# Attention, routing and two feed-forward layers in one kernel: start-up transfers, row numbers and the order of VectorE's work

## The chip, the cores and the metric

The kernel runs on one core of a Trainium2 chip. The metric is the device time of one execution in microseconds, the median of several runs. The engines are TensorE (PE in the profile, its weight loads PEld), VectorE (DVE), ScalarE (ACT), GpSimd (POOL) and SyncE (SP). SP and POOL also issue the DMA transfers, SP on a hardware queue (q1), POOL on a software queue (q0). Each engine carries out its list of instructions in order, and a waiting instruction holds all that stand behind it on its engine.

## What is computed

```python
# attention: 4 x 8 heads, 576 tokens, head size 64
scores = q @ k^T / 8 + min(-(cum_i - cum_j), 0), causal     # cum = cumsum(max(s, 0))
x = softmax(scores) @ v                                     # -> 2304 tokens x 512
# first layer: 8 experts, each takes at most 288 tokens
logits = x @ w_gate                                         # 2304 x 8
for idx in argsort(-logits.flatten()):                      # best pairs first
    give the token to the expert, if the token is free and the expert has room
x[tokens of e] = relu(x[tokens of e] @ w1[e]) @ w2[e]       # 512 -> 1024 -> 512
# second layer
h = x @ w_in                                                # 512 -> 2048
out = (h * sigmoid(1.702 h)) @ w_out                        # 2048 -> 512
```

## The kernel before, in words

**Attention.** The 32 heads go through a pipeline written out by hand in `SEQ`: in step i (`steps`), head i+1 gets its scores (`scores`, L165 and L174), head i its maxima, exponentials and first transposes, head i-1 its product with V (`av`, L228), head i-2 its projection (`fin`, L256). Scores are made of two passes, for more than one float32r's worth of digits. The first uses `X0`: the high part of K (`Ak` on ScalarE, L115, or `k` on POOL, L102) against the high and the low part of Q (`Aq` on ScalarE, L113, and `ql` on POOL, L104). The second uses 68 rows of `X1`: the low part of K (`kl`, POOL, L106), the high part of Q (`Aq1`, or `q1`, a transfer on SP, L108), and four rows 64 to 67 that add the bias: two hold running sums (`c`, two transfers of rows of `c_rows` on SP, L110 and L111) and two hold the constants 1 and -1. There are six such `X1` (`HS`), all in one tile `x1`. The constants are set once for head 0 (L312, L313) and copied to heads 1 to 5 by a POOL transfer (`rest`, L317 and L318). Two more POOL transfers bring `w_gate` into `fold` (L341).

Q and K of two heads are one `load(j)` (four transfers, L79), V of two heads one `load_v(j)` (L85). `prep(i)` issues the V load, `c`, `k`, `kl` and the split of V into a high and a low part (`split_v`, POOL, L91 and L92); `high(i)` issues the rest of head i and, for odd i, the Q and K of a later pair. From head 8 on this is done five steps ahead; the table `HIGH` gives the steps for heads 2 to 7. In the opening block (L304 to L347) the program's order holds on all five engines, in the steps on PE, ACT and DVE; elsewhere the framework's planner orders an engine's list by its own costs and by when it expects an instruction's inputs.

**Routing and experts.** A serial stretch decides which token goes where and leaves the row numbers `ids` (96 x 24). `output_rows` (L768) turns them into rows of the output: `orow` (L769 to L772), converted to whole numbers in `oidx` (L773), written to `o_rows` in memory (L774), and, once program order comes to expert 2, read back transposed as `oids` (128 x 18, L982), as the scatters at the end (L1080) want them. What follows on SP is kept behind the write by `issue_after`. The experts' weights come by `load_w` on SP (L506, L507) and are split on ACT and DVE (L781, L782); `up` (L898) and `down` (L908) multiply; `gather_t` (L873) transposes the gathered tokens of the next expert. Beside them run the conversions of `w_in` and `w_out` from 64-bit numbers (`from_f64`, L803 to L818): a load on SP (L805), then two half conversions on DVE, L808 and L812 (with L811 on ACT), and L814 and L817.

**Feed-forward.** Unit q = 0 to 71 is a chunk of 256 tokens and one of four column pairs; the first 36 units use the first half of the weights. Unit q makes h (`ff_in`, L1013), sg on ACT (L1024), g on DVE (L1025), four sums (L1031), gT's high part on ACT (L1219) and its low part on DVE (L1223). `ff_out` (L1045) multiplies into the banks y0 to y3; while q is below `DEEP` = 30 it does so for unit q-2. After each fourth product `rows_out` empties the banks: p1, p3, p4 are copied by ACT (L1112), and c11, u2, u3, u4, c22 are DVE's (L1076); c11 and u2 need p1. They are placed by slots, run in this order within a deep unit: "B", then g and the sums, gT's high part, "a", "A", gT's low part, "c". The remaining half conversions (`step`) stand in the same slots, one in a unit with p = 1 (that is where a chunk's products end) and two in the others. In the deep part p1 is in "a", c11, u2 and u3 in "A" behind the half conversion, u4 and c22 in "B" of the next unit.

The line that sets the conversions' slots, and the ones that set the sums':

```python
for slot in {1: "A", 2: "BA", 3: "BA", 0: "BA"}[p]:                                        # L1172
at(q, "A", add(c11, c11 if last else p1, P_[2]), add(u2, p1, P_[6]), add(u3, u2, P_[7]))   # L1113
at(q + 1, "B", add(u4, u2, P_[5]), add(c22, c22 if last else u3, P_[5]))                   # L1114
```

Zero matmuls (`pulse`, L691, on a tile `zeros`) already stand in the routing stretch, where TensorE would be idle.

Of the kernel before, what the change touches and what calls it, by code (L numbers as in the profile page):

```python
# [19 lines left out]
I32 = mybir.dt.int32  # L20
# [22 lines left out]
def f32(ap):  # L43
    return ap.bitcast(F32)
# [3 lines left out]
def tile_kernel(ctx, tc, qt, kt, v, s, w_gate, w1, w2, w_in, w_out, out):  # L48
# [33 lines left out]
    def load_v(j):  # L82
        t = att.tile([P, 2, T, D], F32, name="vraw", bufs=3)
        for r in (slice(0, 112), slice(112, P)):
            SY.dma_start(t[r].rearrange("p g t d -> p (g t d)"), v[j, r])  # L85
        st["v", j] = t
# [212 lines left out]
    wg = w_gate.rearrange("(h d) e -> d h e", d=D)  # L299
    sums = consts.tile([P, 5, T, 2], F32, name="sums")  # L300
    warm = consts.tile([1, 2], F32, name="warm")
    G.memset(warm, 0.0)
    with (tc.manual_schedule(engines={PE.engine, A.engine, V.engine, SY.engine, G.engine})):

        SY.dma_start(cs, s)
        first_raw = st["raw", 0] = att.tile([128, 2, 2, SP], F32, name="raw", bufs=3)
        for i in range(2):
            for n, src in ((0, qt), (1, kt)):
                for r in (LO, UP):
                    SY.dma_start(first_raw[r, n, i], src[0, i])  # L310
        A.activation(warm, warm, AF.Exp)
        G.memset(f32(x1[64:68, 0, 0]), 1.0)  # L312
        V.memset(f32(x1[64:68, 0, 1]), -1.0)  # L313
        G.memset(sc, 1.0)
        G.memset(sc[LO, 0:1], 0.125)
        G.memset(sc[UP, 1:2], 0.125)
        rest = f32(x1[64:68, 1:]).rearrange("p i n s -> p i (n s)")  # L317
        G.dma_start(rest, f32(x1[64:68, 0]).rearrange("p n s -> p (n s)")[:, None, :].to_broadcast(list(rest.shape)))  # L318
        G.memset(sums, 1e-9)

        V.tensor_scalar(cs, cs, 0.0, None, op0=OP.max)
        V.tensor_tensor_scan(c_sum, cs, cs, 0.0, op0=OP.add, op1=OP.max)
        A.activation(chl[:, 0], c_sum, AF.Copy)
        V.tensor_scalar(identf, jp, 0.0, None, op0=OP.is_equal)
        V.tensor_tensor(chl[:, 1], c_sum, f32(chl[:, 0]), op=OP.subtract)
        for h in range(2):
            SY.dma_start(f32(X1[h][66:68, 0]), f32(chl[h:h + 1]))
            SY.dma_start(f32(X1[h][64:66, 1]), f32(chl[h:h + 1]))
        SY.dma_start(c_rows, f32(chl))
        for what in ("Aq", "Ak", "Aq1", "Vql", "Vkl"):  # L330
            part(what, 0)
        V.tensor_scalar(identb, jp, 0.0, None, op0=OP.is_equal)
        V.tensor_scalar(maskb, jp, 0.0, -1e9, op0=OP.is_gt, op1=OP.mult)
        for what in ("Aq", "Ak", "Aq1", "Vql", "Vkl"):
            st["prep", 1] = part(what, 1)
        V.tensor_tensor(fold[:, :, :D], identf[:, None, :D].to_broadcast([128, H, D]),
                        identf[:, None, D:].to_broadcast([128, H, D]), op=OP.add)
        load(1)
        load_v(0)
        for g in range(2):  # L340
            G.dma_start(fold[g * D:(g + 1) * D, :, D:], wg)  # L341
        part("c", 2)
        prep(3)
        load(2)
        load_v(1)
        prep(2, False)
        load(3)  # L347

    FN = dict(S=lambda i, u: scores(i, u) if i else scores(0, u, (1,), False), M=row_max, X=exps, T=transp, H=p_hi, L=p_lo, A=av, O=av_out, N=norm, R=recip, F=fin, G=fin_out)

    HIGH = {2: 0, 3: 0, 4: 1, 5: 1, 6: 2, 7: 2}

    def steps(i0, i1):
        for i in range(i0, i1):
# [12 lines left out]
    att_engines.enter_context(tc.manual_schedule(engines={PE.engine, A.engine, V.engine}))  # L367
    for u in (2, 1, 0):
        scores(0, u, (0,))
    steps(-3, 14)  # L370

    zeros = keep.tile([128, 128], BF, name="zeros")
    late = ExitStack()
    late.enter_context(tc.issue_after(st["prep", 17].ins))
    G.memset(zeros, 0.0)
    jrow = rt.tile([128, 128], F32, name="jrow")
    G.iota(jrow, pattern=[[1, 128]], base=0, channel_multiplier=0, allow_small_or_imprecise_dtypes=True)
    pcol = rt.tile([128, 1], F32, name="pcol")
# [380 lines left out]
                fill_slots(False)  # L759


    orow = rt.tile([JS, NC], F32, name="orow")
    late = rt.tile([JS, NC], F32, name="late")
    oidx = keep.tile([JS, NC], I32, name="oidx")
    o_rows = dram.tile([N, 1], I32, name="o_rows")
    oids = keep.tile([128, N // 128], I32, name="oids")

    def output_rows():  # L768
        start = V.scalar_tensor_tensor(orow, ids[:, 1], float(P), ids[:, 0], op0=OP.mult, op1=OP.add)  # L769
        for b in range(1, B):  # L770
            V.tensor_scalar(late, ids[:, 1], float(b * T), float(S - SP), op0=OP.is_ge, op1=OP.mult)
            V.tensor_tensor(orow, orow, late, op=OP.add)  # L772
        V.tensor_copy(oidx, orow)  # L773
        ins = SY.dma_start(o_rows.rearrange("(c p) o -> p (c o)", p=JS), oidx)  # L774
        return start, ins


    JM0, JM, JM7, PM = (3, 3, 4, 4, 5, 5, 7, 7), (1, 1, 3, 3, 5, 5, 7, 7), tuple(m for m in range(1, 9) for _ in range(3)), 5
# [172 lines left out]
    for e in range(E):  # L951
        py = [bank(f"y{d}")[:, :CAP] for d in range(4)]
        hs = {}
        for m in range(10):
            if m < 8:
                if e == m == 0:
                    hs[m] = up(e, m)
                    ctx.enter_context(tc.issue_after(last_lo[0].ins))
                if m % 2 == 0:
                    g = m // 2 + 1  # L960
                    if g < 4:
                        ws[e, g] = weights(e, g)
                    elif e + 1 < E:
                        ws[e + 1, 0] = weights(e + 1, 0)
                if m not in hs:
                    hs[m] = up(e, m)
            if m == 1 and e + 1 < E:
                gather(e + 1)
            for _ in range((JM0 if e == 0 else JM7 if e == E - 1 else JM).count(m)):
                f = next(jobs_, None)  # L970
                if f:
                    f()
            if m == 6 and e + 1 < E:
                gather_t(e + 1)
            if m >= 2:
                down(e, m - 2, hs[m - 2], py)
        for d in range(4):
            A.activation(yt[:, d], py[d], AF.Copy)
        SY.dma_start(y_dram[:, :, e * CAP:(e + 1) * CAP], yt)
        yt = new_yt()  # L980
        if e == 2:
            SY.dma_start(oids, o_rows.rearrange("(c p) o -> p (c o)", p=128))  # L982
        if e in (0, 1):
            for f in load_y(e, wp):
                f()
# [82 lines left out]
    def at(q, slot, *fs):  # L1068
        todo.setdefault((q, slot), []).extend(fs)
# [18 lines left out]
    def rows_out(q, c, acc, last):  # L1088
# [21 lines left out]
            return  # L1110
        for o, k, slot in ((p1, 1, "a"), (p3, 3, "c"), (p4, 4, "c")):
            at(q, slot, lambda o=o, k=k: A.activation(o, P_[k], AF.Copy))  # L1112
        at(q, "A", add(c11, c11 if last else p1, P_[2]), add(u2, p1, P_[6]), add(u3, u2, P_[7]))  # L1113
        at(q + 1, "B", add(u4, u2, P_[5]), add(c22, c22 if last else u3, P_[5]))  # L1114
        if not last:
            at(q + 1, "A", add(c12, u4, p3), add(c21, u3, p4, OP.subtract))
            return
# [43 lines left out]
    with tc.manual_schedule(engines={PE.engine, A.engine, V.engine}):  # L1161
        for q in range(NQ):
# [5 lines left out]
            if p == 0 and 1 <= c < 2 * NCH - 1:  # L1168
                hi, lo = load_y(c + 1, fp)
                at(q + 1, "c", hi)  # L1170
                at(q + 2, "B" if c == NCH - 1 else "A", lo)
            for slot in {1: "A", 2: "BA", 3: "BA", 0: "BA"}[p]:  # L1172
                if q:
                    at(q, slot, lambda q=q: step(q))
            if 0 <= k + 2 < PP:
# [45 lines left out]
                do(q, "a")  # L1221
            do(q, "A")
            V.tensor_tensor(t[:, 1, :n], src, f32(t[:, 0, :n]), op=OP.subtract)  # L1223
            gs[q] = t
            do(q, "c")
        ends.pop()()
# [44 lines left out]
```

## Time and profile before

| what | us |
|---|---|
| median of 3 runs | 897.05 (896.64 to 898.61) |
| the profiled execution | 896.56 |
| its span, first to last instruction | 894.8 |
| mean granted TensorE clock | 0.973 of full speed |
| busy: PE / DVE / ACT / POOL | 840.4 / 723.6 / 509.0 / 276.8 |

The profile is of one execution. Its rows name an engine, a line of the kernel, an operation, the tile written and the tile read, how many such instructions there are and how long they took; brackets tell how long the engine had been idle ahead of the instruction and what ended that. Times of the timeline count from the first instruction. The granted clock is 1.00 for 2.4 GHz and 0.50 for 1.2 GHz.

### The profile page before, as it was taken

What the parts mean: (1) busy time and instruction counts of PE and PEld (TensorE: products, weight loads), DVE (VectorE), ACT (ScalarE), POOL (GpSimd) and SP (SyncE); (2) the same over time, 40 slices, a digit from 0 to 9 for tenths busy, and PEclk for the clock granted to TensorE, in tenths of its full rate; (3) what the DMA queues carried; (4) which work ended last, traced back from release to release, by engine and by line L of the source; (5) the groups of instructions that cost most, each with busy time, mean ns of one, the idle gap of its engine ahead of it and who ended that gap; (6) DMA issues with size and microseconds to landing.
All of it is one profiled execution on the core that took longest, in us unless ns stands there. A gap on an engine that the chain in (4) does not pass through costs nothing.

```text
span 894.8 us, 18574 instructions
## 1 busy us (share of the span) xinstructions
PE 840.4 (94%) x6853; PEld 821.0 (92%) x6853; DVE 723.6 (81%) x1683; ACT 509.0 (57%) x1141; POOL 276.8 (31%) x263
## 2 busy tenths in 40 slices
PE   4799999999669899999999999999999999999996
PEld 3699999999538899999999999999999999999996
DVE  4678889888777689999897798899978977777775
ACT  5889998997534557666664343434335434444442
POOL 2999999983242111021100011111010111111112
PEclk9899999999769999999999999999999999999999
DMA  6886558620346689888874333323256111111101
GB/s 160 193 199 167 149 136 217 156 75 6 123 146 104 226 243 280 258 270 248 258 236 181 99 118 101 118 83 111 73 189 222 56 49 48 48 48 49 48 24 49
DMA packets 88391, 124.38 MB, mean 139 GB/s; under 512 B 10541, under 2 KB 56769, under 8 KB 87781
## 3 DMA queue, kind: packets, MB, share of 16 engines
q1 hardware_dynamic: 85156, 113.55, 43.4%
q0 software_dynamic: 3136, 9.57, 3.7%
q8 instruction: 57, 0.93, 0.4%
q14 instruction: 42, 0.34, 0.1%
HBM read 96.61 MB, written 22.21 MB: 133 GB/s over the span
## 4 chain that ended last, share of the span: by engine, by line
PE 48%; DVE 12%; issue 4%; ACT 3%; DMA 2%; POOL 1%; SPq 0%; POOLq 0%; DVEq 0%; ACTq 0%
PE h L1013 13%; PE y L1045 11%; PE y L908 11%; PE h L898 11%; DVE g L1031 3%; DVE gT L1223 3%; ACT gT L1219 2%; DVE g L1025 2%; DVE part L1076 1%; PE h L873 1%; DVE tmp L1076 1%; DMA wi_dram<-wist 1%; DVE u L814 1%; DMA raw<-in_moe_w_in_dram 1%; DVE yc L941 1%
## 5 line engine op out<-in xcount | busy, mean ns | idle before, releaser
L1013 PE MATMUL h<-yc,win 128*128 128x256 f32 x1728 | 218.6, 283 | 0.0
L1013 PEld LDWEIGHTS h<-yc,win 128*128 128x128 f32 x1728 | 212.4, 192 | 0.0
L1045 PE MATMUL y<-wout,gT 128*128 128x256 f32 x1491 | 189.6, 282 | 7.0 <-DVE part L1076 3.9
L1045 PEld LDWEIGHTS y<-wout,gT 128*128 128x128 f32 x1491 | 180.9, 189 | 9.7 <-issue 4.2
L1219 ACT ACTIVATE gT<-g 128x896 fp32r<-128x896 f32 x72 | 68.4, 950 | 140.5 <-DVE g L1031 139.6
L908 PE MATMUL y<-hT,w2s 128*128 128x288 f32 x768 | 115.8, 299 | 0.0
L898 PE MATMUL h<-xT,w1s 128*128 128x288 f32 (+2 forms) x776 | 114.2, 295 | 0.0
L908 PEld LDWEIGHTS y<-hT,w2s 128*128 128x128 f32 x768 | 107.4, 191 | 0.0
L898 PEld LDWEIGHTS h<-xT,w1s 128*128 128x128 f32 x776 | 106.5, 188 | 0.1
L217 DVE TENSOR_TENSOR phl<-pt,phl 116x464 fp32r<-116x464 f32 (+1 forms) x128 | 76.2, 599 | 28.0 <-ACT phl L212 27.9
L1223 DVE TENSOR_TENSOR gT<-g,gT 128x896 fp32r<-128x896 f32 x72 | 78.9, 1096 | 16.4 <-ACT gT L1219 16.3
L1031 DVE TENSOR_TENSOR g<-g 128x128 f32<-128x128 f32 x284 | 75.2, 306 | 4.9
L228 PE MATMUL pt<-phl,vhl 116*128 116x232 f32 (+2 forms) x512 | 75.7, 291 | 2.4 <-POOL vhl L92 2.1
L212 ACT ACTIVATE phl<-pt 116x464 fp32r<-116x464 f32 (+1 forms) x128 | 69.2, 541 | 12.4 <-PE pt L206 12.1
L670 POOL DMA_INDIRECT xg<-x_rows,idx x24 | 29.3, 1222 | 141.2 <-PE h L873 134.8
L228 PEld LDWEIGHTS pt<-phl,vhl 116*128 116x128 f32 x512 | 66.4, 194 | 4.0 <-POOL vhl L92 2.8
L1080 POOL DMA_INDIRECT out_dram<-part,oids x18 | 22.2, 1231 | 150.5 <-DVE part L1076 150.5
L1020 ACT ACTIVATE sg<-h 128x256 f32<-128x256 f32 x84 | 32.1, 384 | 64.1 <-PE h L1013 63.5
L206 PE MATMUL pt<-identf,pr 116*116 116x116 f32 x480 | 66.7, 271 | 0.9 <-DVE phl L217 0.7
L1021 DVE TENSOR_TENSOR g<-h,sg 128x256 f32<-128x256 f32 x84 | 35.5, 423 | 32.9 <-ACT sg L1020 32.3
L165 PE MATMUL sc<-x 128*116 128x348 f32 (+3 forms) x192 | 44.8, 342 | 16.0 <-ACT x L115 10.4
L206 PEld LDWEIGHTS pt<-identf,pr 116*116 116x116 f32 x480 | 52.5, 143 | 4.4 <-PE sc L174 1.0
(199 smaller groups left out, 1433.6 us busy)
## 6 DMA issues: line engine op xcount, KB each, us to landing
wraw<-in_moe_w_dram SPq DMA_DIRECT2D x60, 512.0 KB
yraw<-y_dram SPq DMA_DIRECT2D x18, 512.0 KB
raw<-in_qt_dram SPq DMA_DIRECT2D x30, 290.0 KB
raw<-in_kt_dram SPq DMA_DIRECT2D x30, 290.0 KB
raw<-in_moe_w_in_dram SPq DMA_DIRECT2D x32, 256.0 KB
raw<-in_moe_w_out_dram SPq DMA_DIRECT2D x32, 256.0 KB
y_dram<-yt SPq DMA_DIRECT2D x8, 576.0 KB
vraw<-in_v_dram SPq DMA_DIRECT2D x16, 280.0 KB
```

The costliest lines, as they stand in the source:

```text
L165: PE.matmul(p[:, c0:c0 + w], X[x][:, 0, t * P:(t + 1) * P], X[x][:, 1, k0:k0 + w], start=x == 0 and banks[m] not in banks[:m], stop=x == 1 ...
L206: PE.transpose(p[:, w - P:w], pr[:, place(t, c):place(t, c + 1)], identf[:P, :P])
L212: A.activation(hl[:, 0], p, AF.Copy)
L217: st["lo", i] = V.tensor_tensor(hl[:, 1], st["pt", i, g], f32(hl[:, 0]), op=OP.subtract)
L228: PE.matmul(p[:, t0 * P:(t0 + n) * P], vhl[:, hh, c].rearrange("p a d -> p (a d)"), st["phl", i, g][:, x, col:col + n * P], start=x == 0 a ...
L898: PE.matmul(p[:, o], w[:, a, k, c], x[:, b, k, o], start=n == 0 and (e, m) != (0, 0), stop=n == len(steps) - 1)
L908: PE.matmul(py[d], w[:, a, m % 2, d * 128:(d + 1) * 128], h[:, b], start=m == 0 and n == 0, stop=m == 7 and n == 2)
L1013: PE.matmul(h, w[:, a, k], yc[c][:, b, k], start=n == 0 and (both is None or half == 0), stop=n == 11 and (both is None or half == 1))
L1031: V.tensor_tensor(g[:, o], g[:, a], g[:, b], op=op)
L1045: PE.matmul(acc[b][:, o * 256:o * 256 + 256], t[:, j, x], wout[:, p, i, y], start=p == 0 and n == 0 and b not in banks[:m], stop=end and n ...
L1219: A.activation(t[:, 0, :n], src, AF.Copy)
L1223: V.tensor_tensor(t[:, 1, :n], src, f32(t[:, 0, :n]), op=OP.subtract)
```

## The change

The constants are now set for two heads at once, and the transfer that copies them to the other four, with the two `w_gate` transfers, stands on POOL behind an element copied from V of pair 0, which it thus waits for. `HIGH` moves heads 3, 5 and 7 by a step. Zero matmuls are put on TensorE in two places, 12 at the start and 6 behind the first pass of head 0. The row numbers stay float32, are transposed on TensorE before they are written and after they are read back (through a spent tile, `lg_all`), and their write stands at expert 0's seventh round, behind `gather_t(1)`. In the feed-forward two slots are added: "e" takes u4 and c22 and "z" takes the half conversion of p = 1, both behind gT's low part; c11, u2 and u3 go to the front of "A".

```diff
+    zeros = keep.tile([128, 128], BF, name="zeros")
+    G.memset(zeros, 0.0)
     G.memset(warm, 0.0)
+    def idle(n):
+        p = ps.tile([P, 512], F32, name="pt", bufs=4)
+        for i in range(n):
+            PE.matmul(p, zeros[:, :P], zeros[:, None, :].to_broadcast([128, 4, 128]), start=i == 0, stop=i == n - 1)
...
         A.activation(warm, warm, AF.Exp)
-        G.memset(f32(x1[64:68, 0, 0]), 1.0)
-        V.memset(f32(x1[64:68, 0, 1]), -1.0)
+        idle(12)
+        G.memset(f32(x1[64:68, 0:2, 0]), 1.0)
+        V.memset(f32(x1[64:68, 0:2, 1]), -1.0)
...
-        rest = f32(x1[64:68, 1:]).rearrange("p i n s -> p i (n s)")
-        G.dma_start(rest, f32(x1[64:68, 0]).rearrange("p n s -> p (n s)")[:, None, :].to_broadcast(list(rest.shape)))
...
         load(1)
         load_v(0)
+        G.tensor_copy(sums[:1, 0, 0, 1:2], st["v", 0][:1, 1, 0, :1])
+        G.memset(sums[:1, 0, 0, 1:2], 1e-9)
+        rest = f32(x1[64:68, 2:]).rearrange("p i n s -> p i (n s)")
+        G.dma_start(rest, f32(x1[64:68, 0]).rearrange("p n s -> p (n s)")[:, None, :].to_broadcast(list(rest.shape)))
         for g in range(2):
             G.dma_start(fold[g * D:(g + 1) * D, :, D:], wg)
         part("c", 2)
...
-    HIGH = {2: 0, 3: 0, 4: 1, 5: 1, 6: 2, 7: 2}
+    HIGH = {2: 0, 3: 1, 4: 1, 5: 2, 6: 2, 7: 3}
...
         scores(0, u, (0,))
+    idle(6)
     steps(-3, 14)
...
-        V.tensor_copy(oidx, orow)
-        ins = SY.dma_start(o_rows.rearrange("(c p) o -> p (c o)", p=JS), oidx)
-        return start, ins
+        return start,
+    def rows_to_dram():
+        p = bank("h")[:NC, :JS]
+        PE.transpose(p, orow, identf[:JS, :JS])
+        V.tensor_copy(o_flat[:NC, :JS], p)
+        SY.dma_start(o_rows.rearrange("(c p) o -> c (p o)", p=JS), o_flat[:NC, :JS])
+    def rows_from_dram():
+        n = N // 128
+        SY.dma_start(o_flat[:n, :128], o_rows.rearrange("(c p) o -> c (p o)", p=128))
+        p = bank("h")[:, :n]
+        PE.transpose(p, o_flat[:n, :128], identf[:n, :n])
+        V.tensor_copy(oids, p)
...
                 gather_t(e + 1)
+                if e == 0:
+                    rows_to_dram()
...
         if e == 2:
-            SY.dma_start(oids, o_rows.rearrange("(c p) o -> p (c o)", p=128))
+            rows_from_dram()
...
-        at(q, "A", add(c11, c11 if last else p1, P_[2]), add(u2, p1, P_[6]), add(u3, u2, P_[7]))
-        at(q + 1, "B", add(u4, u2, P_[5]), add(c22, c22 if last else u3, P_[5]))
+        todo.setdefault((q, "A"), [])[:0] = (add(c11, c11 if last else p1, P_[2]), add(u2, p1, P_[6]), add(u3, u2, P_[7]))
+        at(q if q < DEEP else q + 1, "e" if q < DEEP else "B", add(u4, u2, P_[5]), add(c22, c22 if last else u3, P_[5]))
...
-            for slot in {1: "A", 2: "BA", 3: "BA", 0: "BA"}[p]:
+            for slot in {1: "z" if q < DEEP else "A", 2: "BA", 3: "BA", 0: "BA"}[p]:
...
             V.tensor_tensor(t[:, 1, :n], src, f32(t[:, 0, :n]), op=OP.subtract)
+            do(q, "e")
+            do(q, "z")
             gs[q] = t
             do(q, "c")
```

## Rows read from the trace of the kernel before

**Rows 1.** The page's first part: busy us, share of the span, instructions.

```profile
PE 840.4 (94%) x6853; PEld 821.0 (92%) x6853; DVE 723.6 (81%) x1683; ACT 509.0 (57%) x1141; POOL 276.8 (31%) x263
```

**Rows 2.** Sums by stretch: length, busy by engine, granted clock, DMA share, GB/s.

```profile
20.00:30.00 10.00, 5.34 (x25) 4.55 (x25) 4.11 (x10) 9.28 (x23) 8.80 (x7) 0.73 0.98 223
...
550.00:600.00 50.00, 47.41 (x394) 46.72 (x393) 44.48 (x102) 20.71 (x38) 5.16 (x6) 1.00 0.33 109
```

**Rows 3.** DMA queues in 5.5 to 7.2 us: packets, MB, share of 16 engines.

```profile
q0 software_dynamic: 35, 0.04, 25.9%
q1 hardware_dynamic: 8, 0.01, 1.8%
```

**Rows 4.** DMA issues in 0 to 45 us: KB each, median us to landing.

```profile
x<-x POOLq DMA_DIRECT2D x1, 90.6 KB, 6.7
```

**Rows 5.** Timeline of the attention's first heads: start us, us, engine, line.

```profile
2.44 1.24 SPq L310 DMA_DIRECT2D raw<-in_kt_dram  x2
...
3.71 3.85 SPq L310 DMA_DIRECT2D raw<-in_qt_dram  x2
...
18.47 1.89 SPq L79 DMA_DIRECT2D raw<-in_qt_dram  x2
...
21.05 0.72 POOL L91 CAST vhl<-vraw 116x640 fp32r<-116x640 f32 x1 [1.46 <-DMA vraw<-in_v_dram]
...
24.06 0.71 PE L165 MATMUL sc<-x 128*116 128x348 f32 x4 [2.53 <-POOL x L106]
...
27.67 1.79 PE L228 MATMUL pt<-phl,vhl 116*128 116x348 f32 x6 [2.13 <-POOL vhl L92]
...
42.89 0.55 PE L165 MATMUL sc<-x 68*116 68x348 f32 x3 [2.36 <-DMA x<-c_rows]
...
57.22 0.71 PE L165 MATMUL sc<-x 128*116 128x348 f32 x4
...
63.51 0.71 PE L165 MATMUL sc<-x 128*116 128x348 f32 x4
```

**Rows 6.** The chain that ended last, in order of time: start us, us, what.

```profile
266.59 3.72 DMA xg<-x_rows,idx
...
290.51 4.97 DMA raw<-in_moe_w_in_dram
...
325.64 3.76 PE y L908 x28
```

**Rows 7.** Instructions that write or read x, 14 to 60 us: ns min/median/max.

```profile
L102 POOL TENSOR_SCALAR x<-raw,sc x7: 1723/1734/1744, 27.6 to 59.0; 128x580 fp32r<-128x580 f32 x7
```

**Rows 8.** Timeline of the routing stretch, at a granted clock of 0.50.

```profile
259.60 3.19 PE L691 MATMUL warm<-zeros 128*128 128x512 bf16 x7
```

**Rows 9.** Waits in 255 to 305 us: us in total, times, longest.

```profile
SPq L982 <- DMA o_rows<-oidx: 7.9, 1, 7.9
...
DVE u L808 <- DMA raw<-in_moe_w_in_dram: 6.5, 1, 6.5
...
PE h L873 <- DVE hT L901: 3.3, 1, 3.3
```

**Rows 10.** Timeline behind that last wait.

```profile
297.35 5.48 PE L908 MATMUL y<-hT,w2s 128*128 128x288 f32 x28
```

**Rows 11.** Timeline of VectorE at the first end of a chunk.

```profile
520.36 0.42 DVE L814 SCALAR_TENSOR_TENSOR u<-raw,u 128x256 int32<-128x256 int32 x1
...
521.73 0.42 DVE L1076 TENSOR_TENSOR part<-tmp,y 128x256 f32<-128x256 f32 x1 [0.42 <-ACT tmp L1112]
```

**Rows 12.** Waits of TensorE and of VectorE in 486 to 725 us.

```profile
PE y L1045 <- DVE part L1076: 3.9, 7, 1.1
PE y L1045 <- DVE tmp L1076: 2.5, 4, 0.9
...
DVE g L1025 <- ACT sg L1024: 7.5, 2, 7.1
...
DVE part L1076 <- ACT tmp L1112: 4.5, 7, 1.3
```

More of the change, by code (lines that the diff above doesn't have):

```diff
@@ L369, in tile_kernel @@
         scores(0, u, (0,))
+    idle(6)
     steps(-3, 14)
-    zeros = keep.tile([128, 128], BF, name="zeros")
     late = ExitStack()
     late.enter_context(tc.issue_after(st["prep", 17].ins))
-    G.memset(zeros, 0.0)
     jrow = rt.tile([128, 128], F32, name="jrow")
@@ L759, in tile_kernel @@
                 fill_slots(False)
-    orow = rt.tile([JS, NC], F32, name="orow")
+    orow = keep.tile([JS, NC], F32, name="orow")
     late = rt.tile([JS, NC], F32, name="late")
-    oidx = keep.tile([JS, NC], I32, name="oidx")
-    o_rows = dram.tile([N, 1], I32, name="o_rows")
+    o_rows = dram.tile([N, 1], F32, name="o_rows")
+    o_flat = lg_all.rearrange("p e t -> p (e t)")
     oids = keep.tile([128, N // 128], I32, name="oids")
```

## The prediction

> **What bounds the kernel now.** I began with the page: TensorE is busy for 94% of the span [rows 1], so a gain can only come out of the other 6%, or out of stretches in which TensorE works slowly. The sums by stretch tell where to look [rows 2]: in 20 to 30 us it is busy for 5.34 of 10 us at a granted clock of 0.73, in 550 to 600 us for 47.41 of 50. A third place, behind the gather of expert 1, comes out of the waits (under B). The change touches exactly these three, so there are three terms: A (the start), B (row numbers), C (the deep part of the feed-forward). Between them TensorE's list is full and in order; what is won or lost at one place arrives at the end.
>
> **A, the start: what leaves.** In 5.5 to 7.2 us SP's queue moved 8 packets (0.01 MB) while POOL's software queue moved 35 [rows 3]: the loads of heads 0 and 1 stand still while the copy of the constant rows (L318, 6.7 us to landing [rows 4]) trickles. SP's issues show it too: a pair of loads takes 1.24 us, the pair issued then 3.85 [rows 5]. L318 and L341 leave this place. Bounds of the gain: 0 (the loads were late for another reason) to 3.85 - 1.24 = 2.6; I take 2.6, because the standstill and the long issue fall together, and SP's order passes it on to load(1) and load_v(0). V of pair 0, for which POOL waits until 21.05 [rows 5], then lands at 18.4.
>
> **A: what is added.** Behind that landing POOL makes a one-element copy and a memset (some 0.2), then issues the copy of the rows and the two fold transfers. From issue to landing the copy takes between 3.7 us, as a software gather does in an empty queue [rows 6], and the 6.7 of now; little else is under way then, so 3.7: at 22.3. The Trainium skill (DMA: Bandwidth & Descriptors, Anatomy of one DMA) puts a software transfer at 2.0 us plus bytes over 436 GB/s; for these 74 KB that is an estimate of 2.2 us, which no row here reaches, and the sum below would be 1.5 us better by it.
>
> The new wait is SP's. The bias rows of heads 2 to 5 go into rows that the copy fills, so c(2) must wait for it on SP, and behind c(2) stand c(3), load(2), load_v(1) and load(3). c(2) itself takes between 0 and, again, 3.7 us; with the middle it lands near 24.2. Today TensorE starts head 2 at 24.06, after waiting 2.53 for POOL's kl [rows 5], and comes to the pass that needs c(2) some 0.4 later. So what was won is used up just there: 0, or 3 lost if the copy takes 6.7. load(2) leaves at about 23 instead of 18.47 [rows 5], over 4 late; its first user is head 4.
>
> **A: what moves.** HIGH takes heads 3, 5 and 7 one step later, with their POOL work (k, kl, ql; k alone is 1.73 [rows 7]), their copies on ScalarE, their q1 transfers and load(4) to load(6) on SP. POOL's split of V, for which TensorE waits 2.13 us at 27.67 [rows 5], no longer stands among head 3's copies, and head 4 has one head's copies less ahead of it. Head 2 starts at 24.06 and head 6 at 57.22: 33.2 us for four heads, where one takes 63.51 - 57.22 = 6.3 afterwards [rows 5]. So 8 us are lost there, 2.36 of them at 42.89, where head 4 waits for rows issued behind bulk loads. Bounds: all 8 back, or 4 lost, since load(2) comes that much later and q1 of head 4 may stand behind load(4). I take 3 back: the waits at 27.67 and 42.89, less a part of that lateness.
>
> **A: the zeros.** Seven zero matmuls took 3.19 us at the half clock [rows 8], 0.46 each. The first 12 then cost 5.5 us from about 1.2 us on; TensorE's first use comes after 6.7 even in the new order, so they are covered (without that, under 1 us). The 6 behind head 0's first pass cost up to 2.7 us in front of its second pass; what was won there hides them, or else the later stand at c(2) does. Nor do I credit them: TensorE will idle for some 4 us ahead of c(2), and today the idling ahead of 24.06 and 27.67 went with the lower level, 0.73 in the mean of 20 to 30 us. The longer memsets (two heads for one) lie beside the first loads: 0. **A = -3.0, from -8 to +4.**
>
> **B, the row numbers.** Today o_rows is written, and oids read back, in 2304 pieces of 4 bytes each. SP stands 7.9 us at the read, waiting for the write [rows 9]. Behind it stand expert weights and w_in, issued at 290.51 only and landed 4.97 us later [rows 6]; VectorE waits 6.5 us for w_in, and TensorE 3.3 for VectorE, whose hT (L901) is queued behind it [rows 9]. Then the clock is lower: 28 matmuls take 5.48 us at 297.35 [rows 10] and 3.76 later [rows 6], 1.7 more. Removed: 3.3 + 1.7 = 5.0. Without the stand, SP comes to w_in at 290.5 - 7.9 = 282.6, and it lands at 287.6, ahead of 289, when VectorE runs dry. Next late is VectorE itself, which then has the 6.5 us back for the splits that follow; enough.
>
> Added: two transposes on TensorE and two copies on VectorE for one conversion. The nearest row, a copy of far more elements (yc, part and the like take 0.42 [rows 11]), bounds each at 0.4 from above and 0 from below; I take 0.5 for all. Both new transfers move rows of 384 and 512 bytes, 42 pieces for 4608. TensorE's second transpose waits for a transfer; were that late, the matmuls queued behind it would wait too. **B = -4.5, from -5.0 (nothing added shows) to -1.0 (SP or TensorE waits anew).**
>
> **C, sums ahead of conversions.** Every fourth unit ends a chunk, and TensorE waits for VectorE to empty the four y banks: 3.9 + 2.5 us in seven chunks [rows 12]. The edit moves that unit's half conversion (L814 and L817, or L808 and L812) from ahead of c11, u2, u3 to behind c22. But c11 also waits for p1, which ScalarE copies behind gT's high part. In all 7 chunks VectorE idles for p1 although the conversion runs first, 4.5 us in sum, 1.3 at the longest [rows 12]: the conversion starts at 520.36, is done at 521.31, and c11 starts at 521.73, when p1 ends [rows 11]. So c11 starts no sooner in the new order; VectorE idles through all of the 521.73 - 520.36 = 1.37 us, and the conversion costs its time later. The last chunk has none left (its wait is the 1.3). In the other six, 6 x 1.37 = 8.2 us lie ahead of c11, of which 4.5 - 1.3 = 3.2 are idle: 5.0 us of conversions lose their cover. Has VectorE room for them? From 486 to 725 us L1025 waited twice for sg, that is for a product of TensorE: 7.1 at the start and 0.4 once [rows 12]; its other waits are for ScalarE, inside its own chain. So this chain sets the pace and its added time reaches TensorE: 5.0 - 0.4 = 4.6. u4 and c22 come behind gT's low part as before; only in the last chunk do they pass a gate's product, which gives some tenths back. **C = +4.6, from 0 (absorbed, a gain of tenths included) to +6 (no slack at all, and unit 1 too).**
>
> **Sum.** -3.0 - 4.5 + 4.6 = -2.9, made against the profiled execution (896.56 us), gives 893.7. That execution stands 0.5 under the median of the runs (897.05); I predict for the median: **894.2 us**.
>
> **Rivals.** (1) The conversions are absorbed: VectorE catches up in the units after a chunk, C is 0. For it: a half conversion is a sixth of a unit's time. Against it: that single wait of 0.4 us for TensorE. Time: 897.05 - 3.0 - 4.5 = 889.6. (2) Slower: SP's wait for the copy of the rows. If it takes 6.7 us as now, c(2) comes 3 us later, TensorE stands at head 2, and load(2) to load(4) with q1 of head 4 follow. It decides from about 5 us to landing on. Then A is +4: 897.05 + 4 - 4.5 + 4.6 = 901.2. For it: SP is in order, and the same kind of wait costs 7.9 us in B today; against it: the emptier queue. (3) The wait in B moves instead of going, because the read is again early in SP's order: B = -1.0, 897.7. (4) The start gives all 8 us back, because POOL's work then comes in the order in which the heads need it: 889.2.
>
> **Chances.** The sum 0.40, rival 1 0.25, rival 2 0.20, rival 3 0.10, rival 4 0.05. The sum's own range is 891.5 to 897. 888.5 to 901.0 leaves out the slower half of rival 2 and the edges of rivals 1 and 4, under 2 in 10. A difference below 0.2% (1.8 us) is about what a measurement here can't tell from none. Faster by more, below 895.2: 0.26 of the sum's 0.40, with rivals 1 and 4 (0.29), so 0.55. Within: 0.23, from the sum, rival 3 and the milder end of rival 2. Slower: 0.22.
>
> **What would show it.** A: SP's packets filling 5.5 to 7.2 us; SP waiting at c(2) for the copy; head 6 starting near 54 (57.22 now). B: no wait of SP for o_rows, and TensorE without its stop behind the gather of expert 1. C: VectorE idle for over 1 us ahead of each c11, and TensorE's waits on tmp and part near 11 us instead of 6.4. I am wrong if those waits shrink, or if head 6 starts later than 57.

## The result: 1.3% slower, and the forecast had 0.3% faster

The kernel after takes 908.5 us in the median of four runs (908.3 to 909.4), the kernel before 896.9 beside it (896.6 to 898.6). The ratio is 1.013 with a 95% interval of 1.011 to 1.015. Forecast were 894.2 us, a range of 888.5 to 901.0, and a chance of 0.22 for slower: the time lies 7.5 us above the range.

Two milestones split the loss by the three terms: TensorE's first routing matmul (`acc`), which is the end of the start and of attention, and its first product of the deep feed-forward (`h<-yc,win`). First the kernel before, then the kernel after (TensorE's instructions of one line: ns min/median/max, then first and last start in us):

```profile
L629 PE MATMUL acc<-oh,above x120: 174/176/193, 234.0 to 256.5; 116*128 116x8 bf16 x120
...
L1013 PE MATMUL h<-yc,win x1728: 277/283/283, 490.6 to 879.9; 128*128 128x256 f32 x192
```

```profile
L641 PE MATMUL acc<-oh,above x120: 174/176/193, 244.6 to 267.0; 116*128 116x8 bf16 x120
...
L1038 PE MATMUL h<-yc,win x1728: 277/283/284, 496.8 to 892.2; 128*128 128x256 f32 x192
```

| stretch | before | after | difference | forecast |
|---|---|---|---|---|
| A: to the first routing matmul | 234.0 | 244.6 | +10.6 | -3.0 |
| B: from there to the first deep product | 256.6 | 252.2 | -4.4 | -4.5 |
| C: from there to the span's end (894.8, 906.7) | 404.2 | 409.9 | +5.7 | +4.6 |
| sum | | | +11.9 | -2.9 |

Each column is one profiled execution; how far such milestones scatter is told with the experiments.

### The profile page after: what moved, and what is told of

Read it like the earlier page. It is cut to its first block, busy times and chain, and to the rows that moved or that the text cites. A ratio compares the mean times of both kernels' runs of the same rounds, so it can differ in the third digit from the quotient of the medians.

```text
span 906.7 us, 18618 instructions
## 1 busy us (share of the span) xinstructions
PE 849.1 (94%) x6873; PEld 823.8 (91%) x6873; DVE 724.9 (80%) x1684; ACT 509.5 (56%) x1141; POOL 277.1 (31%) x265
## 4 chain that ended last, share of the span: by engine, by line
PE 44%; DVE 15%; issue 4%; ACT 3%; POOL 1%; DMA 1%; POOLq 0%; DVEq 0%; ACTq 0%
PE h L921 11%; PE y L931 11%; PE h L1038 11%; PE y L1070 10%; DVE g L1056 4%; DVE gT L1248 3%; ACT gT L1244 2%; DVE g L1050 2%; DVE part L1101 1%; PE h L896 1%; DVE u L837 1%; DVE tmp L1101 1%; DVE yc L964 1%; DMA wi_dram<-wist 1%; DVE u L835 1%
## 5 line engine op out<-in xcount | busy, mean ns | idle before, releaser
L1070 PEld LDWEIGHTS y<-wout,gT 128*128 128x128 f32 x1491 | 180.8, 189 | 15.7 <-ACT tmp L1137 10.6
L184 DVE TENSOR_REDUCE nm<-sc 116x1 f32<-116x348 f32 (+2 forms) x96 | 42.6, 472 | 20.3 <-PE sc L174 17.1
```

What stands on the lines that cost most here:

```text
L1070: PE.matmul(acc[b][:, o * 256:o * 256 + 256], t[:, j, x], wout[:, p, i, y], start=p == 0 and n == 0 and b not in banks[:m], stop=end and n ...
```

## The profile after

**The start.** Sums by stretch of the kernel after (columns as in [rows 2]), where 5.34 of 10 and 17.58 of 20 us were busy before:

```profile
20.00:30.00 10.00, 3.38 (x15) 3.33 (x16) 4.02 (x10) 4.36 (x11) 4.66 (x6) 0.59 0.39 77
40.00:60.00 20.00, 10.09 (x51) 8.89 (x50) 6.24 (x15) 9.20 (x26) 17.17 (x12) 0.57 0.85 190
```

The timelines there, of SP at 3.71 us, then of POOL, SP and TensorE:

```profile
3.71 1.24 SPq L319 DMA_DIRECT2D raw<-in_qt_dram  x2
...
18.16 0.18 POOL L349 COPY sums<-vraw 1x1 f32<-1x1 f32 x1
18.31 1.41 POOL L106 TENSOR_TENSOR x<-raw,x 64x580 fp32r<-64x580 f32 x1
19.67 0.09 POOL L350 MEMSET sums<- 1x1 f32 x1
19.71 0.84 POOL L352 DMA_DIRECT2D x<-x  x1
...
24.78 0.22 SPq L110 DMA_DIRECT2D x<-c_rows  x1
...
25.93 1.25 SPq L79 DMA_DIRECT2D raw<-in_qt_dram  x2
...
43.88 0.52 SPq L108 DMA_DIRECT2D x<-x  x1
...
26.62 0.90 PE L165 MATMUL sc<-x 68*116 68x348 f32 x3 [6.66 <-DMA x<-c_rows]
...
49.04 0.90 PE L165 MATMUL sc<-x 68*116 68x348 f32 x3 [5.66 <-DMA x<-x]
...
55.08 1.78 PE L228 MATMUL pt<-phl,vhl 116*128 116x348 f32 x6 [2.50 <-POOL vhl L92]
```

The pair of loads takes 1.24 us (3.85 before). V of pair 0 has landed by 17.5 us (no DMA moves from then to 19.5; forecast 18.4), and POOL comes to it at 18.16, behind head 2's ql. Then POOL takes head 2's kl in between, which the planner had put among the opening block's instructions, the copy of the constant rows is issued at 19.71 only, and SP is let on to c(2) at 24.78. TensorE stands 6.66 us at head 2. load(2) leaves at 25.93, where it left at 18.47 [rows 5]; head 4 waits 5.66 us for its q1, issued at 43.88 behind load(4), and 2.50 for a split of V.

**Row numbers.** The first transfer of w_in leaves SP at 293.74 instead of 290.51 [rows 6], with all the work ahead of it 10.7 us later: 7.4 us gained. SP's timeline:

```profile
293.74 3.39 SPq L828 DMA_DIRECT2D raw<-in_moe_w_in_dram  x2
...
308.91 0.38 SPq L791 DMA_DIRECT2D o_rows<-lg_all  x1
311.62 0.27 SPq L795 DMA_DIRECT2D lg_all<-o_rows  x1
```

SP's wait for o_rows is 2.3 us instead of 7.9 [rows 9], and it stands behind w_in: the write, which left SP at 273.37 before, now leaves at 308.91. The change thus has two parts, long rows and a later place, and no run parts them. The group of TensorE that waited 3.3 us for hT [rows 9] now reads (busy us, mean ns | idle before):

```profile
L896 PE MATMUL h<-identf,xg 96*128 96x96 f32 x96 | 10.0, 247 | 1.2 <-issue 1.1
```

**The deep part.** Waits of TensorE, VectorE and ScalarE in 486 to 745 us (us in total, times, longest), beside [rows 12]:

```profile
PE y L1070 <- ACT tmp L1137: 6.6, 7, 1.0
PE y L1070 <- DVE tmp L1101: 5.2, 7, 1.2
...
DVE part L1101 <- ACT tmp L1137: 9.0, 7, 1.3
...
ACT tmp L1137 <- DVE part L1101: 13.9, 7, 2.1
```

VectorE's idle time ahead of c11 doubled (9.0 us for 4.5), as forecast. TensorE waits 11.8 us on these for 6.4. The last row is new: ScalarE's copies of products 3 and 4, which free the last y banks, wait for c22.

## The experiments

The chips of these runs took 899.9 to 900.4 us in the median for the kernel before (896.1 to 905.6), so ratios to it are compared, and the traces. "Deep part" is the span less the start of the first deep product. Where heads are named, the number is the start of the mask product that closes the head's last score pass, against the kernel before (head 2: 33.45, 5: 56.80, 18: 138.53, 31: 222.89 us):

| kernel | head 2 | head 5 | head 18 | head 31 | ratio, 95% interval |
|---|---|---|---|---|---|
| after | +0.4 | +10.6 | +10.8 | +10.6 | 1.013 (1.011 to 1.015) |
| e1 | -0.1 | +7.4 | +7.5 | +11.3 | 1.009 (1.006 to 1.012) |
| e2 | -4.3 | -0.6 | -0.6 | +0.1 | 1.001 (0.999 to 1.003) |
| e5 | +4.9 | +1.2 | +1.3 | +4.5 | 1.002 (1.001 to 1.004) |
| e6 | -5.5 | -3.1 | -2.9 | +5.5 | 0.996 (0.993 to 0.998) |
| e13 | +7.5 | +3.4 | +3.4 | +3.5 | 0.995 (0.993 to 0.997) |
| e12 | -2.3 | +0.2 | +0.2 | +2.7 | 0.993 (0.991 to 0.996) |
| e9 | -5.7 | -3.1 | -3.0 | -3.2 | 0.987 (0.984 to 0.990) |
| e11 | -4.7 | -2.9 | -2.8 | -4.1 | 0.984 (0.981 to 0.987) |
| e14 | -4.6 | -1.8 | -1.6 | -1.6 | 0.982 (0.979 to 0.984) |
| e15 | -5.6 | -2.8 | -2.6 | -3.7 | 0.983 (0.980 to 0.985) |

One profile of a start is not exact: e4, e7, e8, e10 and e16 have the start of before, and their heads 5 lie between -1.9 and +2.1, their heads 31 between -2.1 and +2.6. e3 has the start of after, and +12.3 and +16.3 there for +10.6 and +10.6. Much of the scatter behind head 28 comes with the range of the logits (told under e6): from head 28 to head 29, where the kernel before takes 8.2 us, the runs with the range in its old place take between 0.5 us less (after) and 3.9 us more (e5), late starts and early ones alike. Differences within that are not read.

### The start: which part cost 10.6 us

**e1**, after with the old head order:

```diff
-    HIGH = {2: 0, 3: 1, 4: 1, 5: 2, 6: 2, 7: 3}
+    HIGH = {2: 0, 3: 0, 4: 1, 5: 1, 6: 2, 7: 2}
```

> The kernel after, with HIGH as it was before; transfers late, zeros, B and C stay. Theory W (the late copy of the constant rows is the root: SP waits for it at c(2) and everything behind comes late): TensorE still stands over 5 us at head 2's second pass and load(2) still leaves near 26 us, so most of the start's +10.6 us stays: 905 to 909 us. Theory H (the new HIGH order is the root: q1 of head 4 stands on SP behind load(4), which waits for its buffer): the 5.7 us stand at head 4 and the 2.5 us for vhl go, the time falls by 6 to 9 us: 900 to 902.5 us.

908.1 us. TensorE stands 4.33 us at head 2 and again at head 4; its timeline:

```profile
49.77 0.90 PE L165 MATMUL sc<-x 68*116 68x348 f32 x3 [5.05 <-DMA x<-c_rows]
```

The wait for q1 is replaced by one for the bias rows. Theory H falls as the root: head 4 is late in either order. In this profile the old order brings head 5 3.2 us sooner than after has it (+7.4), and that is gone by head 31 (+11.3).

**e2**, after with the transfers back at the start:

```diff
+        G.dma_start(rest, f32(x1[64:68, 0]).rearrange("p n s -> p (n s)")[:, None, :].to_broadcast(list(rest.shape)))
         G.memset(sums, 1e-9)
...
+        for g in range(2):
+            G.dma_start(fold[g * D:(g + 1) * D, :, D:], wg)
         load(1)
         load_v(0)
-        G.tensor_copy(sums[:1, 0, 0, 1:2], st["v", 0][:1, 1, 0, :1])
...
-        G.dma_start(rest, f32(x1[64:68, 0]).rearrange("p n s -> p (n s)")[:, None, :].to_broadcast(list(rest.shape)))
-        for g in range(2):
-            G.dma_start(fold[g * D:(g + 1) * D, :, D:], wg)
```

> The kernel after, with the copy of the constant rows and the fold transfers back at the start; HIGH new, zeros, B and C stay. Theory W: SP has no wait at c(2), load(2) leaves near 18.5 us, the start costs nothing or gives up to 3 us: 895 to 899 us. Theory H: q1 of head 4 still comes behind load(4), the stand at head 4 stays: 903 to 907 us.

900.0 us. The whole +10.6 is gone, as far as one profile tells: the first routing matmul stands at 234.0 us as before, the ratio is that of B and C together. Theory W holds.

**e5**, after with SP's order changed:

```diff
-        part("c", 2)
-        prep(3)
         load(2)
         load_v(1)
         prep(2, False)
+        part("c", 2)
+        prep(3)
```

> The kernel after with SP's order at the start changed: load(2), load_v(1) and load_v(2) ahead of c(2) and c(3); the copy of the constant rows stays late. Theory W1 (two halves: the stand at head 2's second pass is the copy's landing itself, the stand at head 4 is load(2)'s lateness): the stand at head 2 stays (6 to 7 us ahead of its second pass), the stand of 5.7 us at head 4 and the wait of 2.5 for vhl go; the start's +10.6 falls to +2 to +4: 900 to 902 us. Theory W2 (head 4 is late because everything behind head 2 is late, whoever loads first): little changes, 906 to 909 us.

902.8 us. As W1 has it: load(2) leaves at 13.18, and head 5 is +1.2 instead of +10.6, though TensorE stands longer at head 2 than expected, for c(2), issued at 28.72 behind a copy that took 8.1 us to landing beside the loads, and for V's split. SP's timeline, then TensorE's:

```profile
13.18 1.25 SPq L79 DMA_DIRECT2D raw<-in_qt_dram  x2
...
30.65 0.90 PE L165 MATMUL sc<-x 68*116 68x348 f32 x3 [9.95 <-POOL vhl L92]
```

So the large part of the loss is not the stand at head 2 but the lateness of what is queued on SP behind the wait. Head 31 has +4.5 again: 3.9 us come at the range, between heads 28 and 29.

**e6**, no copy at all (B and the new start otherwise, deep part as before):

```diff
+        G.memset(f32(x1[64:68, 2:, 0]), 1.0)
+        G.memset(f32(x1[64:68, 2:, 1]), -1.0)
...
-        G.dma_start(rest, f32(x1[64:68, 0]).rearrange("p n s -> p (n s)")[:, None, :].to_broadcast(list(rest.shape)))
...
         prep(2, False)
+        for g in range(2):
+            G.dma_start(fold[g * D:(g + 1) * D, :, D:], wg)
```

> Row numbers' change and the new start, deep part as before; and no copy of the constant rows at all: GpSimd sets them for heads 2 to 5 with two memsets (about 2 us each, beside the first loads), and the fold transfers are issued behind the first split of V. If the copy (landing and SP's wait for it) is what cost the start its 10.6 us, the start is now faster than before's by the 2.6 us of the standstill at least: 886 to 890 us. Rival (the zeros or the new HIGH order cost time by themselves): 892 to 896 us.

896.4 us: a miss, and the most telling one. The two memsets take 2.02 and 2.11 us beside the loads, and heads 5 to 18 come 3 us earlier, the size of the forecast's A. Yet the first routing matmul comes at 239.5, 5.5 later than before. TensorE's timeline, then VectorE's wait of that trace:

```profile
138.62 0.93 PE L165 MATMUL sc<-x 68*116 68x348 f32 x3 [2.18 <-POOL x L106]
...
207.75 0.40 DVE L457 TENSOR_REDUCE rng<-rall 116x2 f32<-116x232 f32 x1 [5.43 <-DMA rall<-rows]
```

Behind that stand of 2.18 us the granted clock is 0.59 in 138 to 141 us and 0.50 in 141 to 144 (1.00 ahead of it), and head 19 comes 2.7 us late where head 18 was 2.9 early. Two things stand in attention's way that the start doesn't touch: POOL is busy for 35 to 39 of every 40 us from 80 to 200 and has over 3 us of constants for the routing among the work around head 17, and the range of the logits goes through memory (written in 4-byte pieces, SP's two issues 9.6 us apart before, 11.8 here).

**e9**, e6 with both eased (the block of constants moves behind the step in which head 27 is prepared, and the range's small sums go along):

```diff
-    late.enter_context(tc.issue_after(st["prep", 17].ins))
+    late.enter_context(tc.issue_after(st["prep", 27].ins))
...
     steps(26, 28)
-    V.tensor_reduce(rng, rall, axis=AX.X, op=OP.max)
...
     steps(28, 29)
+    V.tensor_reduce(rng, rall, axis=AX.X, op=OP.max)
...
     to_grid(0, B - 1)
```

> e6 (row numbers' change, no copy of the constant rows, new start) with the two later stands of attention eased: GpSimd's constants for the routing (some 3.4 us of its time near head 17) come behind the preparation of head 27 instead of 17, and the range of the logits, for which VectorE waited 5.4 us in e6, is used one head later. Theory P (the start did gain 3 us in e6, head 4 to 18 being 2.9 to 3.1 us earlier than before, and lost them where TensorE then waits for GpSimd at head 18 and for the range at head 28): head 31 is now about 3 us earlier than in the kernel before instead of 5.5 later, and the time falls by 5 to 9 us against e6: 888 to 891 us. Rival (GpSimd's pace caps attention as a whole, moving one block only moves the wait): head 31 stays within 1 us of before, 892 to 894 us.

888.4 us, head 31 at -3.2: theory P. The start's 3 us are real, and arrive when these two are out of the way. A smaller lead can pass them as they were: e8 and e10, whose starts happen to have head 5 at -1.3 and -1.9, have head 31 at -1.4 and -2.1.

**e13**, e6 with the copy put back in its place on POOL, into memory that nobody reads:

```diff
+        G.tensor_copy(sums[:1, 0, 0, 1:2], st["v", 0][:1, 1, 0, :1])
+        G.memset(sums[:1, 0, 0, 1:2], 1e-9)
+        G.dma_start(spare, f32(x1[64:68, 0]).rearrange("p n s -> p (n s)")[:, None, :].to_broadcast([4, HS - 2, 2 * SP]))
```

> e6 with a copy of the same size put back at the place on GpSimd where the kernel after has it (behind V of pair 0, with the fold transfers behind it, ahead of V's split), but into spare memory that nobody reads, so that SP's c(2) has nothing to wait for. Theory W (SP's wait does the harm): heads 4 to 18 come no more than 1.5 us later than in e6 (47.4 us at head 4), so still ahead of or level with before (50.5), time 893 to 898 us. Rival (the copy on GpSimd's queue and GpSimd's lost time do it): head 4 at 55 us or later as in after (61.1), time over 901 us.

Between the two: head 4 at 53.5 us (47.4 in e6, 61.1 in after); the time, 896.1 us, is where theory W put it. The copy goes to DRAM here, and beside the loads it takes 6.4 us to landing. SP comes to c(2) at 13.25 us and to load(2) at 15.82, so the wait for the copy is gone, but TensorE has one long stand:

```profile
33.89 1.78 PE L228 MATMUL pt<-phl,vhl 116*128 116x348 f32 x6 [12.02 <-POOL vhl L92]
```

POOL's list isn't written by hand, and here it took later heads' work ahead of the second half of V's split. Without SP's wait +10.6 thus becomes +3.4 at head 5; the 6.5 us that still lie between this and e6 come with the copy's place on POOL, by this stand. What its traffic adds isn't parted from that, and what order POOL's list takes behind a late issue can't be read from the code.

**e12** and **e14**: the zeros and `HIGH` taken out. e12 is e6 without the zeros and with the old `HIGH`, e14 is e15 (below) without `idle(12)` and `idle(6)`.

> e6 without the zeros and with HIGH as before: of the start's change only the copy of the constant rows and the early fold transfers are gone. If the zeros and the new HIGH order were worth the 3 us of e6's heads 4 to 18, these heads come no sooner than in the kernel before; if the copy's traffic was, they come 2 to 3 us sooner (head 4 at 47.5 to 48.5 us, 50.5 before). Time 893 to 897 us either way, since attention's later stands take the gain.

> e15 without the 18 zero matmuls. If the zeros are worth something (they keep TensorE's clock up through the first heads), heads 4 and later come 1 to 3 us later than in e15 and the time is 1 to 3 us longer. As forecast (zeros costed and credited at nothing): heads 4 and later within 0.5 us of e15, the same time, 881.5 to 884 us on a chip where the kernel before takes 897.

e12 has head 5 at +0.2 where e6 has -3.1, and is no slower: 894.1 us, ratio 0.993. e14 takes 884.4 us, e15 883.7. In time neither the zeros nor `HIGH` shows. With the copy and the early fold transfers gone and the start otherwise nearly as before, e12 wins 2.3 us at head 2 and nothing at head 5, so by its expectation e6's 3 us there belong to the zeros or to `HIGH`; e14 speaks against the zeros. But these 3 us are hardly more than starts scatter, and no run has the old `HIGH` with e9's easing, so what the new head order is worth stays open.

### The row numbers

**e4** is the kernel before with B alone (its diff stands ahead of the prediction).

> The kernel before with the row numbers' change alone (two transposes, both transfers in long rows). Theory of the prediction: -4.5 us, by SP's 7.9 us stand gone: 892.5 us, with no stop of TensorE behind the gather of expert 1. Rival (the wait moves, since the read is again early in SP's order): 896 us.

893.9 us against 899.9, ratio 0.994 (0.992 to 0.996), that is 3.8 to 7.6 us. From the first routing matmul to the first deep product it takes 251.9 us (256.6 before), and TensorE's 3.3 us for hT are gone.

### The deep part

**e3** is after with C undone (A and B stay).

> The kernel after, with the deep feed-forward's order as before (C undone), A and B as after. The trace of after puts C at +5.7 us (from the first product of the deep units, 496.8 us, to the end, against 490.6 us before); the prediction had +4.6. If the three terms add up: 902.8 us (prediction's size: 903.9). Rival (the longer start shifts what the deep part meets, and C alone is nothing): 908.5 us.

904.8 us, ratio 1.005 (1.003 to 1.007), with a start still longer than that of after (head 31 at +16.3); deep part 402.5. All seven profiles with the old order of it (before, e3, e4, e6, e9, e12, e13) lie at 402.5 to 404.2, the four others with the new one besides after (e1, e2, e5, e7) at 410.0 to 410.7, and after itself at 409.9. So C costs 5.7 us at the least and 8.2 at the most, by these profiles; by the ratios (1.013 and 1.005) it is some 7. That C alone is nothing falls.

**e7**, B and C on the old start, without the "e" slot:

```diff
-        at(q if q < DEEP else q + 1, "e" if q < DEEP else "B", add(u4, u2, P_[5]), add(c22, c22 if last else u3, P_[5]))
+        at(q + 1, "B", add(u4, u2, P_[5]), add(c22, c22 if last else u3, P_[5]))
```

> Row numbers' and deep part's change on the start of before, but with u4 and c22 at their old place (a unit later, in slot B). With B alone near 892.5 us. Theory of the prediction (the half conversion loses its cover ahead of c11): C stays near +4.6, so about 897 us. Rival (ScalarE's copies of products 3 and 4 now wait for u4 and c22 and so free the y banks late, TensorE's 6.6 us on ScalarE): C falls to +0 to +2, 892.5 to 894.5 us.

900.8 us, ratio 1.000 (0.998 to 1.002); deep part 410.0. ScalarE's wait for c22 is gone, and TensorE's waits are as long as ever, on other works (first row TensorE's group, second VectorE's waits):

```profile
L1058 PE MATMUL y<-wout,gT 128*128 128x256 f32 x1491 | 189.5, 282 | 12.8 <-DVE part L1089 6.2 <-DVE tmp L1089 3.3 <-ACT t L822 2.8
...
DVE part L1089 <- ACT tmp L1125: 9.0, 7, 1.3
```

**e8**, B and C with ScalarE's copy of product 1 first:

```diff
+            do(q, "a")
             t = fp.tile([128, 2, 7, 128], F32R, name="gT", ...)
...
-            if deep:
-                do(q, "a")
             do(q, "A")
```

> Row numbers' and deep part's change on the start of before, and ScalarE's copy of product 1 ahead of gT's high part in the deep units. Theory of the prediction (c11 waits for that copy, so sums first gain nothing): c11 then starts about 0.9 us sooner in each chunk, VectorE's idle time of 1.3 us ahead of it mostly goes, and C falls from +5.7 to between -2 and +2: 890.5 to 894.5 us. Rival (the sums' start is not what counts, VectorE's total load is): C stays at +4 to +6, 896.5 to 898.5 us.

891.7 us, ratio 0.992; deep part 401.1. VectorE no longer waits for product 1. The first half of the forecast's mechanism holds, that c11 hangs on that copy: it was the copy's place that took the sums' early start away.

**e10**, the same edit with the old order of VectorE (B, without C):

> Row numbers' change alone, the deep part in the order of before, but ScalarE's copy of product 1 ahead of gT's high part in the deep units. It tells apart what won in e8 (deep part 401.1 us from its first product to the end, 404.2 before). If the sums' early start is what counts, the half conversion still stands ahead of c11 here, c11 can come at most 0.4 us sooner in each of 7 chunks: -1 to -3 us against B alone, 889.5 to 891.5 us. If the copy's place alone is what counts: as fast as e8, -3 to -4, 888.5 to 889.5.

887.0 us, ratio 0.986 (0.983 to 0.990); deep part 398.7, better than either expectation. Its timeline of VectorE at the first end of a chunk, to be held against [rows 11], and TensorE's group:

```profile
513.70 0.43 DVE L828 SCALAR_TENSOR_TENSOR w<-t,u 128x256 f32<-128x256 f32 x1
514.04 0.41 DVE L1089 TENSOR_TENSOR part<-tmp,y 128x256 f32<-128x256 f32 x1
...
L1058 PE MATMUL y<-wout,gT 128*128 128x256 f32 x1491 | 188.8, 281 | 3.1 <-DVE part L1089 2.6 <-DVE gT L1233 0.4
```

The conversion runs, and c11 follows it without a gap: the wait of [rows 11] for product 1 is gone. Against e4 (deep part 403.6) this one change gives 4.9 us. Seven such waits of at most 0.4 us, as the expectation has them, would give 2.8; what the rest is made of stays open.

**e16**, e8 with e7's edit:

> e8 with u4 and c22 back at their place of before (a unit later). Deep part from its first product to the end: 401.1 us in e8, 398.7 in e10. If ScalarE's copies of products 3 and 4, which now come behind u4 and c22 and on which TensorE waits 3.8 us in e8, are the loss: these waits go, 398 to 399 us. If it is the half conversion's lost cover: 400 us or more.

892.2 us; deep part 401.0: ScalarE's wait for c22 is gone and nothing is won. Sums first costs 2 us even with product 1 copied early (e8 401.1, e16 401.0, e11 400.6 against e10 398.7, e14 399.1, e15 398.6). Why is open: the conversion has no wait for product 1 to hide in there, in either order.

### A version that beats both

**e11** is e9 with e8's deep part, **e15** is e9 with e10's.

> e9 and e8 together: row numbers' change, no copy of the constant rows, late constants and range, sums first with the copy of product 1 ahead of gT's high part. If the parts add up: -3 at the start, -4.9 row numbers, -3 deep part, 885 to 887 us against 897. If the start's gain is lost again in attention: 888.5 to 890 us.

> e9 with e10's edit (the copy of product 1 ahead of gT's high part in the deep units, sums behind the conversion as before). e9's profiled run to the first deep product (483.5 us) and e10's deep part (398.7 us) add up to a span of 882.2 us; against the kernel before: 880 to 884 us where that takes 897, ratio 0.981 to 0.985.

e11 takes 885.1 us, ratio 0.984 (0.981 to 0.987), e15 883.7 us, ratio 0.983 (0.980 to 0.985): by that ratio some 15 us less than the kernel before (0.983 of 896.9). The page's first part of e15, to be held against [rows 1]:

```profile
PE 845.6 (96%) x6873; PEld 823.0 (93%) x6873; DVE 722.5 (82%) x1684; ACT 508.9 (58%) x1141; POOL 281.3 (32%) x264
```

## Why the prediction was wrong

**A, what leaves: right as far as V.** SP's pairs take 1.24 us each, and V lands by 17.5 us, 0.9 ahead of the forecast. That this alone reaches later heads isn't shown (e12: -2.3 at head 2, +0.2 at head 5).

**A, what is added: sized too low.** It read "From issue to landing the copy takes [...] 3.7: at 22.3", c(2) "lands near 24.2", "load(2) leaves at about 23 [...], over 4 late". Shown were: an issue at 19.71 instead of 18.6, since head 2's kl (1.41 us) got in ahead of it; 5.0 us to landing (SP goes on at 24.78); load(2) at 25.93, 7.5 late. The forecast took the lower of its two bounds, a gather in an empty queue [rows 6]; the copy took 5.0 in after, e1 and e3, between that and the early one's 6.7 [rows 4], and in e5, beside loads, 8.1. The Trainium skill (DMA: Bandwidth & Descriptors, Anatomy of one DMA) would give 2.2 us as an estimate; the 5.0 us speak against it for this copy, which reads and writes four partitions only.

**A, what moves: the step that failed.** "I take 3 back" set a gain of `HIGH` against "a part of that lateness", and so priced what stands behind the wait on SP at less than the gain. The lateness decided: 5.66 and 2.50 us of stands at head 4, and a clock of 0.57 around them. Head 6 starts at 67.84 us, where the forecast had named a start behind 57 as a sign that it is wrong. e5 shows the cause (+1.2 for +10.6 at head 5 with load(2) on time); the order of the heads wasn't the root, by e1 and e2. Rival 2 named this wait, its place and the point of 5 us to landing from which it decides; it priced the chain behind it at 4, and it was 10.6. The range ended where that price put it.

**A, the zeros: right.** Costed and credited at nothing; e14 and e15, in which alone they are parted, differ by 0.65 us, within their intervals.

**A premise was wrong as well:** "what is won or lost at one place arrives at the end". A loss did (+10.6 at head 5, +10.6 at head 31). A gain need not: e6 won 3 us and lost them at POOL's pace and at the range's round trip. TensorE's full list [rows 1] hid that POOL was as full in this stretch; the share over the whole span (31%) didn't show it, the sums by stretch did. A gain of A could not be carried to the end without a look at that stretch.

**B: right**, -4.4 for -4.5, and -4.7 from 256.6 to 251.9 in e4. w_in left SP 7.4 us sooner for 7.9. Rival 3's wait is there, 2.3 us long, but the read isn't early any more: it comes behind w_in at 311.62, and TensorE waits for nothing near it. Whether it was the long rows or the later place that helped isn't parted.

**C: the mechanism right, the size 1.1 us short, or more.** VectorE stands ahead of c11 for 9.0 us in seven chunks, TensorE's waits grew from 6.4 to 11.8. e8 shows that c11 hung on ScalarE's copy. That the conversion had its cover there is read from [rows 11] and from the 9.0 us; it isn't all, since sums first costs some 2 us even where nothing waits for the copy (e8, e16 and e11 against e10). The term credited 0.4 us of slack; there was none, and the bound of +6 was nearer. The "e" slot isn't the rest: e7 without it has the same deep part. What the last us are made of stays open. Rival 1 (absorbed) falls.

## What to carry to other kernels

A small copy moved out of the way of bulk loads has to be followed to its waiter: if an in-order queue waits for it, price all that stands behind, at the time at which it would then leave, not the waiter alone. Look in each later stretch for the engine that is full there; an earlier start can be lost where that engine sets the pace. And before work is moved ahead on one engine, ask what its first operand waits for on another: here the copy of one bank, done one instruction earlier, gave 4.9 us of the deep part, where the reordering cost 5.7 or more.

## What the runs showed of the hardware that I had not expected

ScalarE's copy of product 3 waited for VectorE's sum of product 5 (13.9 us in seven chunks after, 6.0 in e8, none in e7, e10 and e16, where u4 and c22 come a unit later): by the code the two share bank y2 and no data. Both also touch the tile `tmp`, but that doesn't make copies wait: in e7, where u2 and u3 are written to it from 521.21 to 522.15 us, the copies start at 521.68. The Trainium skill (PSUM — Partial Sum Buffer, PSUM bank collisions raise a hardware error) asks for PSUM to be guarded by bank and quadrant of partitions, or simply by bank, and not by address, which agrees with this wait; that it is the cause was not tried apart.

The write of 232 numbers in 4-byte pieces held SP's next issue for 9.6 us (188.47 to 198.03 before) and 11.8 in e6, in profiles whose code for it is the same. Other transfers fill the first 4 us of it (0.93 MB in all before), so how much the pieces alone take isn't parted.
